# Gated attention and token mixing on one core: one more block of the symmetric score matrix turned by DMA, and transposing transfers joined in sixteens

## The chip, the cores and the metric

One core of one Trainium2 chip runs the whole kernel. The metric is the device time of one execution in microseconds. Engines are named as the profile names them: PE (TensorE), with its weight loads as PEld, DVE (VectorE), ACT (ScalarE), POOL (GpSimd) and SP (SyncE, which issues most DMAs).

## What is computed

There are 8 batches of 3200 rows. The inputs u and v have 256 columns, z has 64, and the weights w_q, w_k are 256x64, w_out is 256x256.

```
scores = z z^T / S                    S = 3200
attn   = relu(scores)^2
x      = u * (attn v)
wq, wk = x w_q, x w_k
W_tok  = wq wk^T / sqrt(64)
out    = relu(W_tok x) w_out
```

The score matrix of a batch is symmetric. A block of attn for rows of one group and columns of another is the transpose of the block on the other side of the diagonal.

## The kernel before, in words

**Tiles.** A batch has 25 tiles of 128 rows, in seven groups: six of 512 rows and a last one of 128 (`widths`, `starts`). For group `gi` and tile `ti` a score tile of 128x512 is two operands of z on the 64 rows of one half of the array (`scores`, L258). Score tiles are made in pairs, one on each half. A pair fills one PSUM tile of two banks; there are two such PSUM tiles, shared with the projections and the mixing (`ps_tile`).

**Two stages of a pair.** `first_stage` (L278) takes relu from PSUM to SBUF on ACT or DVE (g). `second_stage` (L296) squares g into fp16 on ACT or POOL (at). `second_product` (L345) multiplies at by v on PE into `acc`, four matmuls of 64x256 for a tile and a half group. When a group is complete, `gate` (L361) adds the two accumulators and multiplies by u on POOL; a transposing DMA turns x (L400), `projections` (L413) gives the queries and keys (qk), another transposing DMA turns the keys (kx, L436), POOL doubles them (L448), and `heads` (L450) sums k^T x over the batch. `mix` and `proj` then make the output of the batch while the next batch runs.

**Turned blocks.** `is_turned(b, gi, gj)` (L213) says which blocks are made once: group `gi` makes the tiles of the later group `gj`, and a transposing DMA on SP's queue (`turn` in `second_stage`, L330) writes the transposed block into tt, from which group `gj` takes its weights in place of making the scores again. Turned are blocks with `gj` at most two groups after `gi`, and those with the last group (ttl). Batch 0 leaves one out (`SKIP`); `EXTRA`, a list for batches 1 to 7, is empty. Seven homes hold tt blocks (`NHOME`); a block keeps its home until its last tile is read. A transfer carries what one pair made: eight squares of 128x128, or four where only one tile of the pair is turned. z itself is turned for each next batch by four transfers (`ZTURNS`, L153): seven and six squares, for each of two offsets.

**Order.** No hardware scheduler is involved: the kernel is written out by a planner that runs while the program is built. It keeps a clock for PE, DVE, ACT and POOL, and for SP (`sp_at`) and the DMA engines (`dma_at`), with a cost for every operation, and places the next operation by them (main loop from L1029). `move` (L616) files a DMA with the time from which it may go, a due time, SP's issue time and the DMA time; `send` (L619) issues the one that is due first and says when it will have landed. `use_pair` (L681) makes the next pair of scores when a PSUM tile is free and the pair's at tile can be had; `acc_step` (L955) emits the next matmuls of the second product whose rows are ready by the planner's clock. `add_extra` files projections, mixing and heads. At run time engines meet by semaphores alone, and each engine's and queue's instructions go in the order written. So a wrong cost does not make a wrong result; it makes an engine wait.

**Buffers of the square.** at tiles come from a pool of `NAT` = 16, and pair p may be made when pair p - 16 has been read by all its matmuls and its transfers have landed (L1049, `all_used`).

Of the kernel before, what the change touches and what calls it, by code (L numbers as in the profile page):

```python
# [16 lines left out]
def kernel(  # L17
# [33 lines left out]

    NAT = 16
    NX = 7
# [98 lines left out]
    ztimes = []  # L152
    ZTURNS = [(0, 0, 7), (1, 0, 7), (0, 7, 13), (1, 7, 13)]  # L153

# [55 lines left out]
    SKIP = [(0, 2)]  # L210
    EXTRA = []

# [29 lines left out]
    NPAIR = NTILE // 2  # L242
    made, turned = {}, {}
    NHOME = 7
    homes, homes_free = {}, list(range(NHOME))

# [11 lines left out]
    def scores(p, banks=None):  # L258
        assert len(ztimes) >= 4 * tiles[2 * p + 1][0] and p_chunk(p) in z_at, (p, clock, len(ztimes), z_at)
        sc = banks or ps_tile("sc")  # L260
        for h, (b, gi, ti) in enumerate(tiles[2 * p : 2 * p + 2]):
            gs, gw = starts[gi], widths[gi]
            nc.tensor.matmul(  # L263
                out=sc[h][:, 0:gw] if banks else sc[:, h, 0:gw],
                lhsT=z_cols(b, h, ti * P, P),
                rhs=z_cols(b, h, gs, gw),
                start=True,
                stop=True,
            )
        return sc  # L270
# [25 lines left out]
    def second_stage(p, g, ways):  # L296
        at = pat.tile([P, 2 * W], FP16, tag="at", name="at")
        at0 = 0
        parts = pieces(p)
        if len(ways) > len(parts):  # L300
            parts = [(slice(h, h + 1), parts[0][1]) for h in range(2)]
        for (hs, w), on_act in zip(parts, ways * 2):
            n = hs.stop - hs.start
            out = at[:, at0 : at0 + n * w].rearrange("p (n w) -> p n w", w=w)
            if on_act:
                nc.scalar.square(out=out, in_=g[:, hs, 0:w])  # L306
            else:
                nc.gpsimd.tensor_mul(out=out, in0=g[:, hs, 0:w], in1=g[:, hs, 0:w])  # L308
            at0 += n * w
        at0, blocks = 0, []  # L310
        for tile_ in tiles[2 * p : 2 * p + 2]:
            b, gi, ti = tile_
            made[tile_] = (at, at0)
            gj = group_of(ti)
            if is_turned(b, gi, gj):
                blocks.append((b, gi, gj, ti - starts[gj] // P, 1, at0, at0 + widths[gi]))
            at0 += widths[gi]
        if len(blocks) == 2 and blocks[0][:3] == blocks[1][:3] and blocks[1][3] == blocks[0][3] + 1:
            blocks = [blocks[0][:4] + (2, blocks[0][5], blocks[1][6])]

        def turn(b, gi, gj, n0, nn, c0, c1):
            if (b, gi, gj) not in turned:
# [7 lines left out]
            nc.sync.dma_start_transpose(out=out[:, 4 * n0 : 4 * (n0 + nn), :], in_=at[:, c0:c1])  # L330

        return [(x, lambda x=x: turn(*x)) for x in blocks]
# [266 lines left out]
    mixed_at = []  # L599
    MIXES = 10.0  # L600
    MIXES_END = 14.0
# [7 lines left out]
    LANDS = 4.0  # L609
    RING = 2.0  # L610
    SLACK = 1.0
# [83 lines left out]
    def squares():  # L695
        while pending and pending[0][0] <= clock[PE] + 0.3:
# [7 lines left out]
            else:  # L704
                done = give(ACT, ready, 1.06) if by_act else give(POOL, ready, 1.9)
            for (b, gi, gj, _, nn, _, _), turn in second_stage(p, g, ways):
                n = nn * widths[gi] // P
                due = done + {1: 4.0, 2: 9.0}.get(gj - gi, FARDUE)
                out_of[p] = out_of.get(p, 0) + 1
                move(  # L710
                    done + SLACK, due + SLACK, 1.28, 0.21 * n, turn,
                    lambda t, x=(p, b, gi, gj, nn): block_landed(t, *x),
                    lambda x=(b, gi, gj): has_home(*x),
                )
            for x in tiles[2 * p : 2 * p + 2]:
                row_at[x] = done + 0.6

# [14 lines left out]
    def use_keys(b, gi):  # L732
# [17 lines left out]
        if not final:  # L750
            move(
                done + SLACK, done + 10.0, 1.28, 0.21 * n, lambda: turn_keys(b, gi),
                lambda t: at_time(t, lambda: double(b, gi)),
# [63 lines left out]
    def project_out(b, gi, ps, ready):  # L817
# [25 lines left out]
    def batch_begun(b, t):  # L843
        if b + 1 < B:
            t0 = max(t + 6, Z0)
            at_time(t0, lambda: (load_z(b + 1), push(3.0)))
            step = ZSTEP if b else ZSTEP0
            for i, (_, m0, m1) in enumerate(ZTURNS):
                move(
                    t0 + ZWAIT + step * i, t0 + ZDUE + step * i, 1.28, 0.21 * (m1 - m0),  # L850
                    lambda i=i: turn_z(b + 1, i),
# [6 lines left out]
    def v_loaded(b, n0, nn):  # L858
        load_v(b, n0, nn)
        push(2.5)  # L860
        for n in range(n0, n0 + nn):
            v_at[b, n] = dma_at[0] + 5.0

    z_ready = {}

    def z_here(p):
        b = tiles[2 * p + 1][0]
        return not b or z_ready.get((b, 3), 1e9) <= clock[PE]

    def group_begun(b, gi, t):  # L870
        if gi == 0:
            batch_begun(b, t)
        if gi + 1 < NG:
            move(max(t + 2, clock[POOL] + SLACK), t + 7, 0.55, 1.6, lambda: load_u(b, gi + 1))
        elif b + 1 < B:
            move(max(t + 2, clock[POOL] + SLACK), t + 7, 0.55, 1.6, lambda: load_u(b + 1, 0))

    SPARE = 0.5
    BIAS = 0.2
    XDUE = 5.0  # L880
    XWAIT = 2.0
    LATE = 0.5

    def half_done(b, gi, half):
# [10 lines left out]
        if half == halves(gi)[-1]:  # L895
            n = 8 if widths[gi] == W else 2
            move(
                t + SLACK, t + XDUE, 1.28, 0.21 * n, lambda: turn_x(b, gi),
                lambda t: x_landed(t, b, gi), lambda: len(xTs) < NXT,
# [91 lines left out]

    def all_used(p):
        return all(x in used for x in tiles[2 * p : 2 * p + 2])

# [25 lines left out]
    at_time(V3, lambda: (load_first_v(4, 8), give(POOL, clock[PE], 0.6)))  # L1020
    move(10.0, 14.0, 0.55, 1.6, lambda: load_u(0, 0))
    load_weights()
# [3 lines left out]
    done_acc = 0  # L1026
    lead = 140
    turn_about = False
    while groups or work or current["left"]:  # L1029
# [18 lines left out]
        p = produced[0]  # L1048
        able = p < NPAIR and z_here(p) and z_at[p_chunk(p)] <= now and (p < NAT or all_used(p - NAT) and turned_at.get(p - NAT, 0.0) <= now and not out_of.get(p - NAT))  # L1049
        wanted = able and p * total < (done_acc + lead) * NPAIR  # L1050
# [124 lines left out]
```

## Time and profile before

| | |
|---|---|
| median of 3 runs | 774.61 us (774.49 to 777.17) |
| the profiled execution | 773.15 us |
| its span, first to last instruction | 770.9 us |
| matmuls on PE | 12408 |
| score matmuls (L263) | 924 |
| transposing transfers: tt, ttl, xT, kx, zT | 143, 48, 56, 53, 28 |
| DMA packets | 307114, 141.09 MB |

The profile is one execution. A row of a group names the line, the engine, the operation, what it writes and reads, the count, the busy time in us, the mean of one in ns, and the idle time of the engine just before it with what ended it. A row of the chain is a start, a length and what held the end during that time. A row of a window lists its bounds and its length, and then for PE, PEld, DVE, ACT and POOL the busy time with the count of instructions, the granted clock, the share of DMA time and GB/s. Matmuls overlap in the records, so the mean of one matmul (269 ns for 64x256) is longer than the distance to the next.

### The profile page before, as it was taken

Reading aid. Unit: us, or ns where it says so; the run is one execution under the profiler, and the core shown is the slowest. Engines: PE = TensorE matmul, PEld = TensorE weight load, DVE = VectorE, ACT = ScalarE, POOL = GpSimd, SP = SyncE. Lnnn points to the kernel's source line nnn. Section 1 sums busy time; section 2 is a strip of 40 time slices with the busy share of each in tenths; the row PEclk is TensorE's granted clock in tenths of the full one; section 3 lists DMA queues with packets and bytes.
Section 4 is the critical chain, followed back from the end, with each engine's and each line's share of the span. In section 5 each row is a group of like instructions: output and inputs, shape, how many; then the busy total and the mean of one; then the engine's idle time right before and its main releaser. Section 6 shows DMA issues by size and latency. Waiting matters only on the chain.

```text
span 770.9 us, 28221 instructions
## 1 busy us (share of the span) xinstructions
PE 761.7 (99%) x12408; PEld 678.4 (88%) x12408; DVE 510.5 (66%) x537; ACT 561.2 (73%) x647; POOL 591.1 (77%) x496
## 2 busy tenths in 40 slices
PE   8999999999999999999999999999999999999996
PEld 7889998888898888989889988998889989898884
DVE  6775876675787566765677756765667476675645
ACT  7785876778758678875788677877777676777734
POOL 8796788789687778666778687887878887888740
PEclk9999999999999999999999999999999999999998
DMA  8999999999999999999899999999999998979625
GB/s 199 130 187 182 167 204 173 160 212 194 194 162 189 194 209 190 182 213 203 153 190 162 188 231 163 219 145 160 262 156 192 184 190 211 201 143 203 152 84 191
DMA packets 307114, 141.09 MB, mean 183 GB/s; under 512 B 285744, under 2 KB 288432, under 8 KB 306992
## 3 DMA queue, kind: packets, MB, share of 16 engines
q1 hardware_dynamic: 300224, 123.13, 85.0%
q0 software_dynamic: 6624, 15.98, 14.8%
q8 instruction: 97, 1.59, 0.9%
q14 instruction: 25, 0.20, 0.1%
q10 hardware_dynamic: 144, 0.20, 0.1%
HBM read 59.64 MB, written 26.21 MB: 111 GB/s over the span
## 4 chain that ended last, share of the span: by engine, by line
PE 94%; POOL 2%; DVE 1%; DMA 1%; ACT 1%; issue 1%; POOLq 0%; SPq 0%; DVEq 0%; ACTq 0%
PE acc L351 68%; PE sc L263 13%; PE fo L521 6%; PE qk L417 3%; PE qk L455 2%; POOL at L308 2%; PE mx L483 1%; DMA z<-in_z_dram 1%; POOL x_sb L388 1%; DVE g L290 0%; ACT g L286 0%; DVE fo L546 0%; DMA xT_sb<-x_sb 0%; PE hd L455 0%; ACT at L306 0%
## 5 line engine op out<-in xcount | busy, mean ns | idle before, releaser
L351 PE MATMUL acc<-v_sb,at 64*128 64x256 f16 x7344 | 504.7, 269 | 0.0
L308 POOL TENSOR_TENSOR at<-g 128x1024 f16<-128x1024 f32 (+1 forms) x218 | 402.3, 1859 | 71.6 <-ACT g L286 29.1
L351 PEld LDWEIGHTS <-at 64*128 64x128 f16 x7344 | 407.2, 94 | 48.1 <-issue 4.8
L290 DVE TENSOR_SCALAR g<-sc 128x1024 f32<-128x1024 f32 (+2 forms) x285 | 338.5, 1203 | 122.8 <-PE sc L263 114.3
L306 ACT ACTIVATE at<-g 128x1024 f16<-128x1024 f32 (+2 forms) x255 | 257.2, 1023 | 21.8 <-DVE g L290 17.8
L286 ACT ACTIVATE g<-sc 128x1024 f32<-128x1024 f32 (+2 forms) x186 | 183.2, 989 | 76.8 <-PE sc L263 75.0
L388 POOL TENSOR_TENSOR x_sb<-both,u_sb 128x512 f16<-128x512 f32 (+1 forms) x112 | 135.8, 1217 | 81.6 <-DVE both L369 77.7
L263 PE MATMUL sc<-zT 64*128 64x512 f16 x924 | 188.1, 375 | 1.4 <-DVE g L290 0.6
L351 PE MATMUL acc<-v_sb,tt 64*128 64x256 f16 x2272 | 163.4, 269 | 0.0
L351 PEld LDWEIGHTS <-tt 64*128 64x128 f16 x2272 | 126.2, 94 | 10.3
L369 DVE TENSOR_TENSOR both<-acc,both 128x512 f32<-128x512 f32 (+1 forms) x104 | 69.6, 670 | 21.4 <-ACT both L368 17.0
L263 PEld LDWEIGHTS <-zT 64*128 64x128 f16 x924 | 61.2, 94 | 7.6 <-issue 3.9
L368 ACT COPY both<-acc 128x512 f32<-128x512 f32 (+1 forms) x69 | 39.0, 565 | 38.7 <-PE acc L351 36.1
L546 DVE TENSOR_SCALAR fo<-fo 128x1024 f32<-128x1024 f32 (+1 forms) x28 | 32.4, 1166 | 46.6 <-PE fo L521 46.6
L509 ACT ACTIVATE rt<-mx 128x1024 f16<-128x1024 f32 x39 | 39.9, 1024 | 12.6 <-PE mx L483 12.1
L521 PE MATMUL fo<-wo,rt 128*128 128x256 f16 x386 | 46.6, 273 | 0.5 <-ACT rt L505 0.5
L521 PEld LDWEIGHTS <-rt 128*128 128x128 f16 x386 | 36.2, 98 | 8.4 <-issue 3.6
L431 ACT CAST qk<-qk 128x512 f16<-128x512 f32 (+1 forms) x47 | 25.3, 539 | 24.6 <-PE qk L455 20.0
L368 DVE COPY both<-acc 128x512 f32<-128x512 f32 (+1 forms) x35 | 23.6, 674 | 21.2 <-PE acc L351 19.9
L470 DVE TENSOR_TENSOR ha<-qk,ha 128x512 f32<-128x512 f32 x37 | 25.5, 689 | 14.4 <-ACT qk L431 14.1
L551 ACT ACTIVATE fo<-fo 128x1024 f32<-128x1024 f32 (+2 forms) x23 | 22.5, 978 | 16.5 <-PE fo L521 15.8
L417 PE MATMUL qk<-xT_sb,wqk 64*128 64x256 f16 (+1 forms) x404 | 32.3, 265 | 0.0
(55 smaller groups left out, 282.9 us busy)
## 6 DMA issues: line engine op xcount, KB each, us to landing
u_sb<-in_u_dram SPq DMA_DIRECT2D x48, 512.0 KB, 4.8
out_dram<-fo SPq DMA_DIRECT2D x46, 512.0 KB, 5.1
v_sb<-in_v_dram POOLq DMA_DIRECT2D x35, 320.0 KB, 6.0
zn<-in_z_dram POOLq DMA_DIRECT2D x7, 400.0 KB, 7.8
tt<-at SPq DMA_TRANSPOSE x143, 4.7
u_sb<-in_u_dram SPq DMA_DIRECT2D x8, 128.0 KB, 2.9
out_dram<-fo SPq DMA_DIRECT2D x4, 256.0 KB, 3.3
xT_sb<-x_sb SPq DMA_TRANSPOSE x56, 5.4
```

The source lines that it names most:

```text
L263: nc.tensor.matmul(out=sc[h][:, 0:gw] if banks else sc[:, h, 0:gw], lhsT=z_cols(b, h, ti * P, P), rhs=z_cols(b, h, gs, gw), start=True, st ...
L286: nc.scalar.activation(out=g[:, hs, 0:w], in_=part, func=RELU, scale=GSCALE)
L290: nc.vector.tensor_scalar(out=g[:, hs, 0:w], in0=part, scalar1=0.0, scalar2=GSCALE, op0=AOP.max, op1=AOP.mult,)
L306: nc.scalar.square(out=out, in_=g[:, hs, 0:w])
L308: nc.gpsimd.tensor_mul(out=out, in0=g[:, hs, 0:w], in1=g[:, hs, 0:w])
L351: nc.tensor.matmul(out=accs[half, r][:, ds((j % 2) * D, D)], lhsT=weights(b, gi, ti, j)[top(r), :], rhs=vs[b][top(r), ti, :], start=(first ...
L368: copy(out=both[:, 0 : n * D], in_=accs[half, 0][:, 0 : n * D])
L369: nc.vector.tensor_add(out=both[:, 0 : n * D], in0=accs[half, 1][:, 0 : n * D], in1=both[:, 0 : n * D])
L388: nc.gpsimd.tensor_mul(out=xs[b, gi][:, 0:n, :, r, :].rearrange("p n c d -> p (n c) d"), in0=both[:, 0 : n * D].rearrange("p (m d) -> p m ...
L417: nc.tensor.matmul(out=ps[:, r, 0 : n * P], lhsT=wqk[top(r), c, :, :].rearrange("p t h -> p (t h)"), rhs=xTs[b, gi][top(r), 0:n, c, :], st ...
L509: nc.scalar.activation(out=out, in_=part, func=RELU)
L521: nc.tensor.matmul(out=banks[r][:, ds(j * D, D)], lhsT=flat[:, ds((dc * n + j) * P, P)], rhs=wo[:, dc, :], start=(dc == 0 and j == 0), sto ...
```

## The change

- `EXTRA` names block (1, 4): in batches 1 to 7 group 1 makes the tiles of group 4 (the second and the fifth groups), a transfer turns them, and group 4 no longer makes the tiles of group 1.
- Where two pairs that follow each other hold the four tiles of one turned block, they share one at tile of double width, and one transfer of sixteen squares is issued after both are squared. The pool is 10 single tiles and 3 double ones in place of 16 single ones. `prior` says for each pair which earlier pairs must be done with (`has_at` takes the place of `all_used`).
- z is turned by two transfers of thirteen squares in place of four.
- The planner's costs are redrawn: a transposing transfer of n squares takes 0.2 + 0.13 n in place of 0.21 n of DMA time, and so on as in the diff. `XWAIT`, `MIXES`, `lead`, `V1` and `BIAS` are set anew.

```diff
-    NAT = 16
+    NAT = 10
+    NAT2 = 3
...
-    ZTURNS = [(0, 0, 7), (1, 0, 7), (0, 7, 13), (1, 7, 13)]
+    ZTURNS = [(0, 0, 13), (1, 0, 13)]
...
-    EXTRA = []
+    EXTRA = [(1, 4)]
...
+    def block_of(p):
+        rows = [(b, gi, group_of(ti)) for b, gi, ti in tiles[2 * p : 2 * p + 2]]
+        b, gi, gj = rows[0]
+        whole = rows[0] == rows[1] and is_turned(b, gi, gj) and gj < LASTG
+        return rows[0] + (tiles[2 * p][2] - starts[gj] // P,) if whole else None
+
+    twos, prior, at_of, done_at = {}, {}, {}, {}
+    ones = []
+    for p in range(NPAIR):
+        x, y = block_of(p), block_of(p + 1) if p + 1 < NPAIR else None
+        if p - 1 in twos:
+            continue
+        if x and y and x[:3] == y[:3] and (x[3], y[3]) == (0, 2):
+            pairs = sorted(twos)
+            prior[p] = (pairs[-NAT2], pairs[-NAT2] + 1) if len(pairs) >= NAT2 else ()
+            twos[p] = p + 1
+        else:
+            prior[p] = (ones[-NAT],) if len(ones) >= NAT else ()
+            ones.append(p)
...
     def second_stage(p, g, ways):
-        at = pat.tile([P, 2 * W], FP16, tag="at", name="at")
-        at0 = 0
+        if p in twos:
+            at = pat.tile([P, 4 * W], FP16, tag="ats", name="at", bufs=NAT2)
+            at_of[p], at_of[p + 1] = (at, 0), (at, 2 * W)
+        elif p not in at_of:
+            at_of[p] = pat.tile([P, 2 * W], FP16, tag="at", name="at"), 0
+        at, first = at_of[p]
+        at0 = first
...
+        if p in twos:
+            blocks = []
+        elif p - 1 in twos:
+            blocks = [blocks[0][:3] + (0, 4, 0, 4 * W)]
...
-    MIXES = 10.0
+    MIXES = 14.0
...
-    RING = 2.0
+    VLANDS = 4.0
+    RING = 1.5
...
         begun = max(sp_at[0], clock[PE])
-        dma_at[0] = max(dma_at[0], begun) + takes
         sp_at[0] = max(begun + issue, dma_at[0] - RING)
+        dma_at[0] = max(dma_at[0], begun + max(issue, 0.9)) + takes
         if landed:
-            landed(max(sp_at[0], dma_at[0]) + LANDS)
+            landed(dma_at[0] + LANDS)
...
-                    done + SLACK, due + SLACK, 1.28, 0.21 * n, turn,
+                    done + SLACK, due + SLACK, 1.25, 0.2 + 0.13 * n, turn,
...
-        move(done + SLACK, done + 6.0, 0.55, 1.6, stores[0], landed)
+        move(done + SLACK, done + 6.0, 0.45, 1.7, stores[0], landed)
...
-        dma_at[0] = max(dma_at[0], clock[PE]) + takes
+        dma_at[0] = max(dma_at[0], clock[PE] + 2.0) + takes
...
-    V1 = 10
+    V1 = 8
...
-            at_time(t0, lambda: (load_z(b + 1), push(3.0)))
+            at_time(t0, lambda: (load_z(b + 1), push(2.4)))
...
-        push(2.5)
+        push(2.0)
         for n in range(n0, n0 + nn):
-            v_at[b, n] = dma_at[0] + 5.0
+            v_at[b, n] = dma_at[0] + VLANDS
...
-    BIAS = 0.2
+    BIAS = 0.0
     XDUE = 5.0
-    XWAIT = 2.0
+    XWAIT = 7.0
...
-    lead = 140
+    lead = 150
```

The issue and DMA costs of the other transposing transfers, the loads of u and the stores change in the same way.

More of the change, by code (lines that the diff above doesn't have):

```diff
@@ L258, in scores @@
     def scores(p, banks=None):
-        assert len(ztimes) >= 4 * tiles[2 * p + 1][0] and p_chunk(p) in z_at, (p, clock, len(ztimes), z_at)
+        assert len(ztimes) >= len(ZTURNS) * tiles[2 * p + 1][0] and p_chunk(p) in z_at, (p, clock, len(ztimes), z_at)
         sc = banks or ps_tile("sc")
@@ L309, in second_stage @@
             at0 += n * w
-        at0, blocks = 0, []
+        at0, blocks = first, []
         for tile_ in tiles[2 * p : 2 * p + 2]:
@@ L867, in z_here @@
         b = tiles[2 * p + 1][0]
-        return not b or z_ready.get((b, 3), 1e9) <= clock[PE]
+        return not b or z_ready.get((b, len(ZTURNS) - 1), 1e9) <= clock[PE]
     def group_begun(b, gi, t):
@@ L990, in p_chunk, with has_at @@
         return max(c for c, (n0, nn) in enumerate(ZCH) for i in t if n0 <= i < n0 + nn) if p < 12 else 3
-    def all_used(p):
-        return all(x in used for x in tiles[2 * p : 2 * p + 2])
+    def has_at(p):
+        return all(
+            all(x in used for x in tiles[2 * q : 2 * q + 2])
+            and turned_at.get(q, 0.0) <= clock[PE]
+            and not out_of.get(q)
+            for q in prior.get(p, ())
+        )
     blank = wo[:, 0, 0:P]
@@ L1048 @@
         p = produced[0]
-        able = p < NPAIR and z_here(p) and z_at[p_chunk(p)] <= now and (p < NAT or all_used(p - NAT) and turned_at.get(p - NAT, 0.0) <= now and not out_of.get(p - NAT))
+        able = p < NPAIR and z_here(p) and z_at[p_chunk(p)] <= now and has_at(p)
         wanted = able and p * total < (done_acc + lead) * NPAIR
```

17 lines of the change are left out of this document (10 added, 7 removed).

## The prediction

> **What bounds the kernel now.** I read first the share of each engine and the granted clock on the profile's page, then the windows of 100 us, then the list of who waited for whom on TensorE, then the chain that ended last.
>
> ```profile
> span 770.9 us, 28221 instructions
> PE 761.7 (99%) x12408; PEld 678.4 (88%) x12408; DVE 510.5 (66%) x537; ACT 561.2 (73%) x647; POOL 591.1 (77%) x496
> PEclk9999999999999999999999999999999999999998
> ...
> PE 94%; POOL 2%; DVE 1%; DMA 1%; ACT 1%; issue 1%; POOLq 0%; SPq 0%; DVEq 0%; ACTq 0%
> ```
> ```profile
> 100.00:200.00 100.00, 100.00 (x1651) 87.84 (x1649) 65.58 (x70) 75.48 (x84) 84.09 (x70) 1.00 1.02 189
> ...
> 600.00:700.00 100.00, 100.00 (x1650) 91.54 (x1646) 66.68 (x67) 73.96 (x85) 82.60 (x69) 1.00 0.96 187
> 700.00:771.00 71.00, 64.54 (x966) 53.40 (x962) 38.92 (x46) 39.10 (x56) 35.51 (x27) 0.97 0.59 151
> ```
>
> TensorE is busy for 99% of the span at the full granted clock, and from 100 to 700 us it has no hole. "Busy" alone does not say that the matmuls run at their best rate, so the next rows are from the chain: stretches between 30 and 36 us.
>
> ```profile
> 30.46 4.37 PE acc L351 x80
> 34.83 0.22 PE sc L263 x2
> 35.05 0.55 PE acc L351 x10
> 35.59 0.22 PE sc L263 x2
> ```
>
> 80 matmuls of the second product take 4.37 us, 0.0546 us each, and two score matmuls (one pair, on the two row halves) take 0.22 us. About 1650 matmuls stand in each window of 100 us, a mean of 0.061 us with the longer score and projection matmuls in it. So the stream is packed, and the number of matmuls sets the time. Two places are not packed, the first 52 us and the last 25 us. The chain at 45 to 52 us shows the first:
>
> ```profile
> 45.51 0.23 PE sc L263 x2
> ...
> 46.88 1.06 ACT at L306
> 47.93 0.92 ACT g L286
> 48.85 0.04 issue
> 48.90 0.41 PE sc L263 x2
> ```
> ```profile
> PE sc L263 <- DVE g L290: 0.6, 2, 0.4
> PE fo L521 <- ACT rt L505: 0.5, 1, 0.5
> PE ztp L130 <- POOL zd L124: 0.4, 1, 0.4
> PE sc L263 <- ACT g L286: 0.3, 1, 0.3
> PE qq L417 <- DMA xT_sb<-x_sb: 0.2, 1, 0.2
> ```
>
> The second fence is the list of waits on TensorE (its first row, 1.0 us for the memset before the warm-up, is left out). No matmul waits for a transposed block anywhere, and for a DMA only 0.2 us, at the end.
>
> **The change, part by part.**
>
> *The block of groups 2 and 5.* Until now rows 1 and rows 4 (counted from 0) each compute their half of the block. From batch 1 on, group 1 makes it, a transposing transfer turns it, and group 4 reads the result. That drops 4 tiles of 128x512 in each of 7 batches: 28 score matmuls, 14 pairs. In the changed program's order TensorE has 896 score matmuls instead of 924, and all its other matmuls in the same numbers. 14 pairs by 0.22 us from the chain is **3.1 us** less on the engine that sets the end.
>
> ```profile
> L308 POOL TENSOR_TENSOR at<-g 128x1024 f16<-128x1024 f32 x211 | 396.5, 1893 | 70.0 <-ACT g L286 29.1 <-DVE g L290 29.0 <-issue 9.6
> L290 DVE TENSOR_SCALAR g<-sc 128x1024 f32<-128x1024 f32 x278 | 335.2, 1221 | 121.8 <-PE sc L263 113.3 <-POOL at L308 3.3 <-ACT g L286 1.8
> L306 ACT ACTIVATE at<-g 128x1024 f16<-128x1024 f32 x240 | 250.8, 1056 | 21.8 <-DVE g L290 17.8
> ```
>
> The same 14 pairs leave the other engines: 14 evictions of some 1.2 us and 14 squares of 1.06 us (ScalarE) or 1.89 us (GpSimd), at most 14 x (1.22 + 1.89) = 44 us. These engines stand at 66 to 77% and nothing on TensorE ends later for it, so I count nothing.
>
> *Seven more turned blocks, sixteens, and z in two.* Here are the transfers as they are, by tile: issue on SP and issue to landing, shortest, median and longest.
>
> ```profile
> L330 SPq DMA_TRANSPOSE tt<-at x143: 1231/1354/5576, 17.1 to 713.4; - x143
> ...
> DMA to landing us min/median/max: 2.4/4.7/9.8
> ```
> ```profile
> L330 SPq DMA_TRANSPOSE ttl<-at x48: 1193/1262/2715, 26.4 to 723.4; - x48
> ...
> DMA to landing us min/median/max: 2.3/4.7/9.3
> ```
> ```profile
> L436 SPq DMA_TRANSPOSE kx<-qk x53: 1182/1233/2294, 50.2 to 733.7; - x53
> ...
> DMA to landing us min/median/max: 2.3/4.0/9.4
> ```
>
> The order has 251 transposing transfers instead of 328: 80 on tt (77 of sixteen 128x128 squares) for 143, 14 on z for 28, the rest unchanged. 77 issues fewer by 1.3 us is about 100 us less on SP's queue. It is off the path. The squares themselves rise by 7 x 16 = 112.
>
> A transfer of 16 is in no row. From 4 squares (ttl) to 8 (tt) the shortest issue goes from 1.19 to 1.23 us and the shortest landing from 2.3 to 2.4 us, with equal medians of 4.7 us. So one end for a sixteen is no difference, the other is twice an eight: 2.7 us of issue and 9.4 us at the median. I take a value near the first, since the step from 4 to 8 is nearly flat.
>
> Perfetto Trace Analysis in the Trainium skill, section What "DMA-bound" means, says that the DMA slice on the issuing engine's track is descriptor generation, not movement of data. If that grew with the squares, the sixteens would save no time on SP, and the estimate of 100 us there would fall to about nothing. The rows for 4 and 8 speak against such growth, and no row here shows 16. By that rule rival 3 below would weigh about twice as much; the sum is the same, since SP is off the path.
>
> What hides these transfers is distance in TensorE's order. I counted matmuls in the changed program from the last score matmul behind a transfer to the first matmul that reads it. The shortest for a sixteen after batch 0 is 421 matmuls, by 0.0546 us 23.0 us; in the program before the shortest for an eight outside the first two blocks is 471, 25.7 us. The chain to hide is an eviction (1.2), a square (1.9), the other pair's square (1.9 if behind it), an issue and a landing: 9.7 us at the median landing, 14.8 us at the longest of 9.8 us, and 19.8 us if the median doubles and two issues of 2.7 us stand ahead. All are under 23.0 us, so **0**. In batch 0 one sixteen has 327 matmuls, 17.9 us (there an eight had 313 before), which holds up to the longest landing. If the cover is gone, TensorE waits for the difference, once per block.
>
> A joined transfer waits for both pairs' squares, and SP's queue is in order: keys, x, u and stores behind it start later. x has its cover enlarged (a wait of 7 instead of 2 in the planner). The keys are the one whose cover shrinks: the shortest distance from a projection to the first matmul on its turned keys is 273 matmuls before and 191 now, 14.9 and 10.4 us; the median goes from 369 to 331.
>
> ```profile
> L448 POOL COPY kx<-kx 128x128 f16<-128x128 f16 x92 | 24.0, 291 | 2.2 <-DMA kx<-qk 2.2
> L431 ACT CAST qk<-qk 128x512 f16<-128x512 f32 x40 | 23.4, 586 | 23.0 <-PE qk L455 18.5 <-PE qk L417 4.2
> ```
>
> Their chain is a cast of 0.6 us, the landing of 4.0 us (9.4 at the longest) and two copies of 0.3 us: 5.2 us, 10.6 us at worst, without time in queues. I take 0 and keep this as the rival on the slow side.
>
> *Buffers.* 16 square tiles become 10 plus three double ones, the same space. A too small pool would show as ScalarE or GpSimd waiting for TensorE; now the square's largest idle cause is the eviction (29.1 and 29.0 us above). With 44 us of work less I count nothing.
>
> *Redrawn clocks and the first 52 us.* The planner's new costs move the order. What can press TensorE is a pair of PSUM tiles: I looked for places where a PSUM tile is written again less than 1.0 us after it was filled, between 12 and 715 us. There are 14 before and 13 now, seven of them in each between two projections. Four score matmuls in a row at 46 us are the place of the gaps shown above; the list of waits from 40 to 56 us and the group of half squares price it:
>
> ```profile
> PEld L263 <- issue: 1.5, 4, 0.6
> ```
> ```profile
> L308 POOL TENSOR_TENSOR at<-g 128x512 f16<-128x512 f32 x5 | 5.2, 1040 | 0.0
> ```
>
> The weight loads of the scores wait 1.5 us there in four gaps. In the new order that spot is gone, and two like it stand at 19.7 and 20.6 us of matmul time. I count 0.55 us for each, near the longest gap of 0.6. The balance is 1.1 - 1.5 = **-0.4 us**. Its bounds are -1.5 (nothing new) and +1.7: GpSimd does two more half squares before its first gating, and 2.1 us for them could all be exposed.
>
> *The tail* has the same operations in the same sequence: 0.
>
> **Sum.** 3.1 + 0.4 = 3.5 us. The profiled execution took 773.15 us (span 770.9 and 2.25 around it), the median of the three runs is 774.61, 1.46 above. 773.15 - 3.5 = 769.65 us; carried to the median, **771.1 us**. That is 0.45% and just inside 0.5% (3.9 us), which is about what a measurement of this kernel can tell from no change.
>
> **The rivals.**
>
> 1. *More comes back.* The chain gives 6% of the span to others than TensorE, mostly at start and end. If none of the new tight spots at the start costs anything (-1.5 in place of -0.4) and the relieved engines and queue free another 1.0 us there, the time is 771.1 - 2.1 = 769.0 us. For it: GpSimd is the chain at the start. Against: the end is unchanged.
>
> 2. *The gain is used up.* DMA is what becomes tighter.
>
> ```profile
> DMA  8999999999999999999899999999999998979625
> ...
> q1 hardware_dynamic: 300224, 123.13, 85.0%
> ```
>
> The DMA digits are 9 almost throughout. All of q1's 655 us put on its 2130 or so squares gives at most 0.31 us a square, 34 us of DMA for 112 more, against nothing if 4 and 8 cost alike. It stays hidden as long as the distances above hold. If a tenth of it, 3.5 us, comes out at TensorE, the time is 774.6 us.
>
> 3. *Slower: the keys come late.* A key transfer behind two sixteens with doubled issues (5.4 us), landing at the longest (9.4), takes 0.6 + 5.4 + 9.4 + 0.6 = 16.0 us. A quarter of the 53 key blocks, 13, are read within 15.8 us of TensorE's work in the new order. If these are late by 1 us on average, the time is 771.1 + 13 = 784 us. It begins to decide where a key's chain passes 10.4 us and turns the sign where the waits sum to 3.5 us. Against it: 5.2 us is the chain at the median, and SP has fewer issues.
>
> That the change does not do what it says is excluded by the order: 28 score matmuls fewer, 77 sixteens.
>
> **How the numbers follow.** Forecast 0.55 (own range 770.0 to 773.2, by the bounds of the start), rival 1 0.18, rival 2 0.15, rival 3 0.12. Faster by over 0.5% (below 770.7): rival 1 and a third of the forecast, which has half its weight between 770.0 and 771.1: 0.18 + 0.18 = 0.36. Within: the other 0.37 of the forecast and rival 2, 0.52. Slower: 0.12. The range leaves out rival 3 and some of rivals 1 and 2 at their edges: 768.3 to 776.0 us.
>
> **What would show it.** Right: score matmuls x896; TensorE still at 100.00 in the windows from 100 to 700 us; no wait of TensorE on tt or kx; key and tt landings near 4 to 6 us; sixteens' issue near 1.3 us. Wrong: TensorE waiting on kx or on L448's copies (rival 3), an issue of 2.7 us for a sixteen, or gaps in the first 30 us larger than those now at 46 us.

## The result, and the profile after

| | before | changed |
|---|---|---|
| median of 22 runs each, side by side | 775.22 us (773.12 to 780.77) | 780.66 us (775.11 to 794.35) |
| ratio | | 1.0057, 95% interval 1.0031 to 1.0083 |
| profiled execution, its span | 773.15, 770.9 us | 791.02, 789.2 us |

The changed kernel is slower by 0.57%, over the 0.5% of the forecast's cases and outside its range: rival 3 of the prediction is the case that came. Medians are of all executions, while a ratio leaves out those more than 1.5% above the fastest of the same kernel: the traced ones of the changed kernel (ten microseconds above its median) and of e17 below are among these, and e17's ratio rests on two of six. So the trace of the changed kernel says where time can go, and the sizes are taken from the ratios of the experiments.

This is the page of the changed kernel. Against the rows shown of before, the count of matmuls is 28 lower as forecast; TensorE's share falls from 99% to 97%, the fifth slice of the granted clock is 7, and the chain that ended last leaves TensorE for 12% of the span in place of 6%.

```profile
span 789.2 us, 27992 instructions
...
PE 764.2 (97%) x12380; PEld 666.6 (84%) x12380; DVE 491.8 (62%) x527; ACT 545.1 (69%) x624; POOL 597.8 (76%) x503
...
PEclk9999799999999999999999999999999999999999
...
PE 88%; issue 4%; POOL 3%; DVE 2%; DMA 2%; ACT 1%; SPq 0%; POOLq 0%; DVEq 0%; ACTq 0%
```

These are the windows of TensorE alone (bounds, length, busy time and count, granted clock, DMA share, GB/s). Before held 1553 matmuls in the first 100 us and about 1650 in each of the next six. The packed stream now has holes, by far the largest in the first window: 212 matmuls fewer, some 13 us at 0.061 us.

```profile
0.00:100.00 100.00, 88.25 (x1341) 0.95 0.99 157
100.00:200.00 100.00, 100.00 (x1676) 1.00 1.10 187
200.00:300.00 100.00, 97.39 (x1582) 0.98 1.04 185
...
600.00:700.00 100.00, 98.36 (x1624) 1.00 1.04 193
```

These rows say who waited, on TensorE and then on GpSimd (sum, times, longest). Before had no such rows on TensorE, and 2.2 us in two waits where GpSimd now has 47.4 in twelve.

```profile
PE qk L485 <- POOL kx L478: 5.1, 3, 3.8
PE sc L284 <- issue: 4.6, 1, 4.6
PE acc L381 <- POOL at L334: 4.2, 2, 2.6
```
```profile
POOL kx L478 <- DMA kx<-qk: 47.4, 12, 13.6
```

The timeline shows the first of them whole (start, length, engine, line, with the idle time before it in brackets):

```profile
67.58 10.85 SPq L360 DMA_TRANSPOSE tt<-at  x1
...
78.52 1.38 SPq L360 DMA_TRANSPOSE ttl<-at  x1
...
79.99 1.26 SPq L466 DMA_TRANSPOSE kx<-qk  x1
...
86.86 0.52 POOL L478 COPY kx<-kx 128x128 f16<-128x128 f16 x2 [13.63 <-DMA kx<-qk]
...
87.21 1.03 PE L485 MATMUL qk<-x_sb,kx 64*128 64x256 f16 x8 [3.83 <-POOL kx L478]
```

One sixteen holds SyncE for 10.85 us, the keys' transfer goes out behind it, GpSimd stands 13.6 us in front of the copies that double the keys, and TensorE, out of other work, waits for the copies. Now the transfers by tile, to set beside those of before (tt 143 issues of 1231/1354/5576 ns, landing 2.4/4.7/9.8 us; kx landing 2.3/4.0/9.4):

```profile
L360 SPq DMA_TRANSPOSE tt<-at x80: 1254/2827/10847, 16.7 to 729.8; - x80
...
DMA to landing us min/median/max: 2.4/5.8/18.4
```
```profile
L466 SPq DMA_TRANSPOSE kx<-qk x53: 1161/1223/2846, 53.1 to 752.8; - x53
...
DMA to landing us min/median/max: 2.3/4.6/9.3
```

The median issue of a sixteen (a transfer of sixteen squares) is 2.8 us, twice that of an eight. The keys' own transfer is hardly slower than before. What makes the keys late stands ahead of them.

### The profile page after: what moved, and what is told of

The parts are those of the page before. It is cut to its first block, busy times and chain, and to the rows that moved or that the text cites. A ratio compares the mean times of both kernels' runs of the same rounds, so it can differ in the third digit from the quotient of the medians.

```text
span 789.2 us, 27992 instructions
## 1 busy us (share of the span) xinstructions
PE 764.2 (97%) x12380; PEld 666.6 (84%) x12380; DVE 491.8 (62%) x527; ACT 545.1 (69%) x624; POOL 597.8 (76%) x503
## 4 chain that ended last, share of the span: by engine, by line
PE 88%; issue 4%; POOL 3%; DVE 2%; DMA 2%; ACT 1%; SPq 0%; POOLq 0%; DVEq 0%; ACTq 0%
PE acc L381 64%; PE sc L284 12%; PE fo L551 5%; PE qk L447 3%; PE qk L485 2%; POOL at L334 2%; PE mx L513 1%; DVE g L311 1%; DMA kx<-qk 1%; POOL x_sb L418 1%; DMA z<-in_z_dram 1%; ACT g L307 0%; DVE fo L576 0%; DMA xT_sb<-x_sb 0%; DVE both L399 0%
## 5 line engine op out<-in xcount | busy, mean ns | idle before, releaser
L381 PE MATMUL acc<-v_sb,at 64*128 64x256 f16 x7120 | 489.9, 269 | 4.3 <-POOL at L334 4.2
L334 POOL TENSOR_TENSOR at<-g 128x1024 f16<-128x1024 f32 (+2 forms) x225 | 409.7, 1834 | 65.1 <-DVE g L311 50.4
L311 DVE TENSOR_SCALAR g<-sc 128x1024 f32<-128x1024 f32 (+1 forms) x282 | 334.5, 1193 | 190.9 <-PE sc L284 187.9
L381 PEld LDWEIGHTS <-at 64*128 64x128 f16 x7120 | 387.0, 94 | 58.7 <-POOL at L334 5.1
L332 ACT ACTIVATE at<-g 128x1024 f16<-128x1024 f32 (+2 forms) x236 | 238.9, 1027 | 34.8 <-DVE g L311 31.0
L381 PE MATMUL acc<-v_sb,tt 64*128 64x256 f16 x2496 | 186.8, 272 | 0.0
L381 PEld LDWEIGHTS <-tt 64*128 64x128 f16 x2496 | 140.0, 95 | 16.4 <-issue 1.1
L284 PEld LDWEIGHTS <-zT 64*128 64x128 f16 x896 | 59.2, 94 | 11.8 <-issue 7.4
L581 ACT ACTIVATE fo<-fo 128x1024 f32<-128x1024 f32 (+2 forms) x44 | 41.8, 997 | 29.4 <-PE fo L551 29.3
L478 POOL COPY kx<-kx 128x128 f16<-128x128 f16 (+1 forms) x99 | 25.6, 288 | 47.4 <-DMA kx<-qk 47.4
L539 ACT ACTIVATE rt<-mx 128x1024 f16<-128x1024 f32 x36 | 36.8, 1023 | 15.3 <-PE mx L513 15.3
L485 PE MATMUL qk<-x_sb,kx 64*128 64x256 f16 x348 | 29.2, 273 | 5.1 <-POOL kx L478 5.1
```

Of the source, the lines that this page charges most:

```text
L284: nc.tensor.matmul(out=sc[h][:, 0:gw] if banks else sc[:, h, 0:gw], lhsT=z_cols(b, h, ti * P, P), rhs=z_cols(b, h, gs, gw), start=True, st ...
L311: nc.vector.tensor_scalar(out=g[:, hs, 0:w], in0=part, scalar1=0.0, scalar2=GSCALE, op0=AOP.max, op1=AOP.mult,)
L381: nc.tensor.matmul(out=accs[half, r][:, ds((j % 2) * D, D)], lhsT=weights(b, gi, ti, j)[top(r), :], rhs=vs[b][top(r), ti, :], start=(first ...
L485: nc.tensor.matmul(out=ps[:, r, D : 2 * D], lhsT=ks[b, gi][top(r), n, :, :].rearrange("p a h -> p (a h)"), rhs=x_rows(b, gi, n)[top(r), :, :],
L581: nc.scalar.mul(out=flat_out[:, sl], in_=part, mul=FINAL_SCALE)
```

## The experiments

Three theories stand at the start. **K**: the new order leaves the keys too little cover, and they come late. **D**: joined transfers make DMA late as a whole. **B**: the added block is too much for DMA. Later ones are named where they enter. Cover is counted in the written order, in matmuls from a keys' projection (with the heads written right behind it) to the first heads matmul on these keys: fewest 273 and median 369 before, 191 and 331 in the changed kernel.

**e1: more cover for the keys**

```diff
-                lambda t: at_time(t, lambda: double(b, gi)),
+                lambda t: at_time(t + 4.0, lambda: double(b, gi)),
```

> The changed kernel, with the doubling of the turned keys on GpSimd filed 4 us later in the planner (and so the heads that read them). Theory K (the keys land late behind sixteens on the in-order SP queue; GpSimd waits for them in its own order, TensorE starves): the waits of GpSimd for the keys, 47.4 us in the changed kernel's profile, fall under 10 us, TensorE's waits for the copies (5.1 us) go, and the time falls from 780.7 to 771 to 775 us. Theory D (DMA as a whole is late since sixteens hold its rings): other waits stay, time 777 to 782 us. Theory B (the added block is too much traffic): unchanged, 780 us.

Measured: 773.48 us against 776.2 for before in the same session, ratio 0.9987 (0.9960 to 1.0013); cover 255 and 387. The wait on the keys is down to 0.4 us in one time, and TensorE's longest wait is of another kind:

```profile
  DMA kx<-qk: 0.4, 1
```
```profile
PE sc L284 <- ACT g L307: 2.8, 3, 2.1
```

One number in the planner takes back all of the loss, 0.70% or 5.4 us between the two ratios. K holds so far. The sixteens are as slow to issue as in the changed kernel (median 2836 ns on tt), so their slowness alone does not cost the time.

**e2: each sixteen as two eights, same order**

```diff
-            nc.sync.dma_start_transpose(out=out[:, 4 * n0 : 4 * (n0 + nn), :], in_=at[:, c0:c1])
+            for i in range(max(1, nn // 2)):
+                m, c = (2, (c1 - c0) // 2) if nn == 4 else (nn, c1 - c0)
+                nc.sync.dma_start_transpose(
+                    out=out[:, 4 * (n0 + m * i) : 4 * (n0 + m * i + m), :],
+                    in_=at[:, c0 + c * i : c0 + c * i + c],
+                )
```

> The changed kernel with the same order on every engine, each transfer of sixteen squares issued as two of eight directly behind each other. Theory D (the size of a transfer matters by itself): time falls to 771 to 775 us, landings of tt near 4.7 us, the longest issue under 6 us. Theory K: SP holds as long (two issues of 1.3 us or more for one of 2.8), so 778 to 784 us, GpSimd still waits 30 us or more for keys. Theory B: 780 us.

Measured: 794.41 us, ratio 1.0202 (1.0164 to 1.0239). D falls: unjoined, the same order is much worse. K's wait came (55.3 us on the keys), but its time is a miss by 10 us. The time of DMA packets is a little longer than in the changed kernel, which has the same order and the same squares (e2 first):

```profile
q1 hardware_dynamic: 314560, 126.80, 85.5%
```
```profile
q1 hardware_dynamic: 312096, 126.79, 84.9%
```

0.855 of 791.5 us is 677, 0.849 of 789.2 us is 670. The other nine orders with the block and sixteens have 645 to 663 us, so orders differ by more than these two runs do. What makes e2 slower than the changed kernel by their ratios was not shown.

**e3: without the added block**

```diff
-    EXTRA = [(1, 4)]
+    EXTRA = []
```

> The changed kernel without the added block (EXTRA empty), so 28 score matmuls and 3.1 us of TensorE more, 7 sixteens less. Theory B (112 more squares saturate DMA): the waits go and the time is 774 to 776 us. Theories K and D: sixteens and new clocks stay, so waits stay and the time is 780 to 785 us.

Measured: 782.44 us, ratio 1.0071 (1.0043 to 1.0099). B falls: without the block the kernel isn't faster. Its trace has the same stall at the keys:

```profile
POOL kx L478 <- DMA kx<-qk: 21.7, 8, 5.9
```
```profile
PE qk L485 <- POOL kx L478: 2.6, 1, 2.6
```

**e4: the old clocks under the new transfers.** All costs and settings of the planner are put back; sixteens, z in two and the block stay.

```diff
-    MIXES = 14.0
+    MIXES = 10.0
-                    done + SLACK, due + SLACK, 1.25, 0.2 + 0.13 * n, turn,
+                    done + SLACK, due + SLACK, 1.28, 0.21 * n, turn,
...
```

> The changed kernel with sixteens, z in two and the added block, but all planner costs and settings as before (0.21 us a square, the later landing, waits of 2 for x, lead 140 and so on). Theory K in the form that the redrawn clocks took the cover from the keys: time 771 to 775 us. Theory D (sixteens by themselves): 778 us or more.

Measured: 816.36 us, ratio 1.0521 (1.0489 to 1.0552), a miss for K, and within D's open range (778 or more) by its time but not by its reason. The keys wait only 3.8 us in it. The order itself has the holes: run through as the kernel writes it, the planner's own clock of PE stands at 813.7 when the last operation is placed, against 756.9 in the changed kernel and 760.6 in before. At 0.21 us a square it believes a sixteen to hold DMA for 3.4 us, and delays the rows. The clocks can't be parted from the transfers that they describe.

**e8: the redrawn clocks alone**, in the kernel before.

```diff
-    MIXES = 10.0
+    MIXES = 14.0
-                    done + SLACK, due + SLACK, 1.28, 0.21 * n, turn,
+                    done + SLACK, due + SLACK, 1.25, 0.2 + 0.13 * n, turn,
...
```

> The kernel before with all the redrawn clocks, and no more: transfers of eight, z in four, the old set of blocks. The fewest matmuls between a keys' projection and its first use fall to 183 (191 in the changed kernel, 273 before). Theory K+S (the keys come late only where a short cover meets a transfer of sixteen ahead of them on the queue): GpSimd's wait for the keys' transfer stays under 15 us in sum, the time is that of before within 0.5%, 773 to 779. Rival C (the short cover is enough by itself): that wait is over 30 us as in the changed kernel, and the time 779 to 783. Rival E (the redrawn clocks are a gain of their own that the sixteens ate): 769 to 772.

Measured: 794.15 us, ratio 1.0231 (1.0182 to 1.0279). K+S, that the keys need a sixteen ahead to be late, falls: eights do it too. It is rival C, the short cover by itself, and 11 us dearer than the upper end of C's figure. The loss is not planned (the planner's clock ends at 760.1). The clocks alone take the cover to 183, GpSimd waits as in the changed kernel, and TensorE waits 9.7 us for the copies:

```profile
POOL kx L448 <- DMA kx<-qk: 53.5, 15, 7.0
```

**e5: the added block alone**, in the kernel before.

```diff
-    EXTRA = []
+    EXTRA = [(1, 4)]
```

> The kernel before with the added block and nothing else: transfers of eight, z in four, the old clocks. 28 score matmuls fewer and 14 transfers of eight more. The fewest matmuls of the keys are 231 (273 before). If the block is worth its matmuls in any frame (the changed kernel's part that was right): 771 to 773, 3 us under before. Theory S in its form for eights (more transfers hold the queue too): part or all of it comes back, 774 to 777. If the old frame has no DMA room left at all: over 778.

Measured: 790.98 us, ratio 1.0190 (1.0150 to 1.0229): outside the first two cases, in the last one by its time. Whether the chip's DMA had no room was not tested. The keys wait 5.2 us in it. As in e4 the planner writes the holes itself (its clock ends at 780.8), and the windows lose a little everywhere:

```profile
200.00:300.00 100.00, 98.16 (x1600) 1.00 1.10 191
300.00:400.00 100.00, 98.12 (x1630) 1.00 1.09 188
400.00:500.00 100.00, 97.64 (x1572) 1.00 1.08 196
```

So no part that was run alone is a gain: block alone +1.9%, clocks alone +2.3%, transfers and block without clocks +5.2%, all together +0.6%. The sixteens alone and z in two alone were not run.

**e9, e10, e11: e1 without the block (second edit), and e1 with 2 us (shown) and 8 us in place of 4**

```diff
-                lambda t: at_time(t + 4.0, lambda: double(b, gi)),
+                lambda t: at_time(t + 2.0, lambda: double(b, gi)),
-    EXTRA = [(1, 4)]
+    EXTRA = []
```

> The changed kernel with the keys' doubling filed 4 us later, as in e1, and without the added block. Theory K+S: with the keys' stall gone the block is worth its 28 score matmuls in full, so this is 3.1 us over e1, 776 to 777. Rival F (tensor-engine work is not what the end waits for even then; e1 gained by something else): the time is that of e1 within 1 us, 773 to 774.5.

> The changed kernel with the keys' doubling filed 2 us later, half of e1. The fewest matmuls are 219 (191 in the changed kernel, 255 in e1). Theory K+S: the stalls shrink with the cover: GpSimd's wait for the keys' transfer falls from 47 us to between 5 and 25, the time lies between e1 and the changed kernel, 774.5 to 778. Rival R (e1 was a luckier order, the cover has nothing to do with it): wait and time don't follow the cover, 779 or more is as likely as less.

> The changed kernel with the keys' doubling filed 8 us later, twice e1. The fewest matmuls are 301. Theory K+S: the stall is gone at 4 us already, so nothing more comes of it: no wait for keys among the largest, the time that of e1 within 2 us, 772 to 775.5. Rival R: as with 2 us, any time between 773 and 783. Rival G (every matmul of cover is worth something, since transfers of 18 us occur): 769 to 772.

Measured: e9 777.14 us, ratio 1.0015 (0.9990 to 1.0040); e10 778.51, 1.0019 (0.9985 to 1.0053); e11 779.87, 1.0055 (1.0020 to 1.0090). The block's 28 matmuls, forecast at 3.1 us, are worth 2.2 us by the ratios of e9 and e1, each known to some 2 us; so this agrees with the forecast without showing it. e10 lies between as K has it, with 17.7 us of waits on the keys (its median is half a microsecond above the range given). e11 is a miss. Its plan is longer (the planner's clock ends at 760.9, against 757.0 in e1). It has no wait on the keys, but one stall of another kind near 330 us, where the square's tiles were not free because sixteens had not landed:

```profile
POOL at L334 <- DMA tt<-at: 9.6, 3, 5.6
ACT at L332 <- DMA tt<-at: 8.1, 1, 8.1
```

More cover at the keys than needed brings nothing, and the late sixteens then show at another place. This is what theory S took up: the planner charges a sixteen's issue with 1.25 us and it takes 2.8, so whatever has the shortest cover behind it is late. Its rival R is that each order draws a stall or two of its own by chance.

**e13, e12, e15: the true issue charged (first edit); the same with e1; e1 with a longer landing (second edit)**

```diff
-                    done + SLACK, due + SLACK, 1.25, 0.2 + 0.13 * n, turn,
+                    done + SLACK, due + SLACK, 1.25 if n < 16 else 2.8, 0.2 + 0.13 * n, turn,
-    LANDS = 4.0
+    LANDS = 6.0
```

> The changed kernel, where the planner charges SyncE 2.8 us for the issue of a sixteen (the traced median is 2.83) in place of 1.25, and nothing else. The fewest matmuls from a keys' projection to their first use become 233 (191 in the changed kernel, 255 in e1, 219 in e10). Theory S (the queue of SyncE is held by sixteens for longer than the planner knows, and whatever has the shortest cover is then late: the keys in the changed kernel, squares' buffers in e11): the order leaves more room behind sixteens, GpSimd's wait for the keys' transfer falls under 20 us, time 773 to 777. Rival R (each order draws its own one or two stalls by chance): any time between 773 and 783. Rival K (only the filed cover of the keys counts): as e10 by its distance, 776 to 779.

> e1 (keys' doubling filed 4 us later) with the true 2.8 us issue of a sixteen charged too. The fewest matmuls of the keys are 279 (255 in e1). Theory S: no stall of TensorE over 3 us anywhere, time 771 to 774, at or under e1. Theory K: as e1, 773.5. Rival R: 773 to 783.

> e1 with the landing of every transposing transfer assumed 6 us after its place in the planner's DMA clock in place of 4. The fewest matmuls of the keys are 287. Theory S: like e12, more room for all transfers, 771 to 774. Theory K: as e1, 773.5. Rival R: 773 to 783.

Measured: e13 777.15 us, ratio 1.0024 (0.9995 to 1.0052), keys' wait 22.5 us; e12 775.40, 1.0010 (0.9984 to 1.0037), 4.8 us; e15 775.39, 1.0016 (0.9983 to 1.0050), 11.4 us. The true charge helps by itself, to the edge of what S gave in time and just past it in the wait (under 20 us); K's 776 to 779 by the cover of 233 holds it as well. With e1 neither charge adds anything: e12 and e15 are over the figures of S and of K, and R alone is not excluded by them. Planned room has a price in these orders (the planner's clock ends at 759.9 in both, against 757.0 in e1).

**e17, e18: the keys earlier in SyncE's queue, without and with e1's cover** (2 us in e18)

```diff
-                done + SLACK, done + 10.0, 1.25, 0.2 + 0.13 * n, lambda: turn_keys(b, gi),
+                done + SLACK, done + 6.0, 1.25, 0.2 + 0.13 * n, lambda: turn_keys(b, gi),
```

> The changed kernel where the keys' transfer is due 6 us after its cast in place of 10, so that the planner places it further ahead in SyncE's queue, and nothing else. The cover stays as short as in the changed kernel or shorter: fewest matmuls 191 (191), median 307 (331). Theory Q (the late keys are time in SyncE's queue behind other transfers): the median wait from the cast to the issue falls under 3 us from 3.8, the longest under 13 us from 17.8, GpSimd's wait for the keys' transfer falls well under 47 us, time 774 to 778. Theory K (the cover decides, the queue does not matter): wait and time as in the changed kernel or worse, 780 to 785. Rival R (every order has one or two stalls of its own): 773 to 783, with the largest stall at another tile.

> e1 (keys' doubling filed 4 us later) with the keys' transfer due 2 us after its cast in place of 10. The fewest matmuls of the keys are 249 (255 in e1), the median 391 (387). Theory Q: queue short and cover long, no wait for keys worth naming; the block's 3.1 us comes out against the kernel before: 770 to 773. Theory K: as e1, 772 to 775. Rival R, or the other transfers pushed back by the keys come late in their place: 775 to 783.

Theory Q is that the late keys are time in SyncE's queue behind other transfers. Measured: e17 791.56 us, ratio 1.0086 (1.0055 to 1.0117); e18 782.66, 1.0054 (1.0023 to 1.0086). Q's figures are missed: in e17 the median wait ahead of the keys' issue did fall, to 2.9 us, but the longest was 15.9 (under 13 was expected), and with the cover as short as in the changed kernel GpSimd waits as long as there. As the longest waits stayed, e17 doesn't show what a short queue would do.

```profile
  DMA kx<-qk: 48.7, 15
```

e18 has the cover and still one large stall. Its timeline on SyncE, GpSimd and TensorE, and the windows of TensorE around it:

```profile
328.60 16.49 SPq L360 DMA_TRANSPOSE tt<-at  x2
...
345.20 2.06 SPq L466 DMA_TRANSPOSE kx<-qk  x1
...
349.19 0.52 POOL L478 COPY kx<-kx 128x128 f16<-128x128 f16 x2 [9.01 <-DMA kx<-qk]
...
349.54 1.03 PE L485 MATMUL qk<-x_sb,kx 64*128 64x256 f16 x8 [5.79 <-POOL kx L478]
```
```profile
338.00:342.00 4.00, 4.00 (x58) 1.00 1.35 69
342.00:346.00 4.00, 1.75 (x32) 1.00 1.28 108
346.00:350.00 4.00, 0.46 (x6) 0.79 0.97 105
350.00:354.00 4.00, 4.00 (x40) 0.50 1.01 223
354.00:358.00 4.00, 4.00 (x63) 0.85 1.08 148
358.00:362.00 4.00, 4.00 (x72) 1.00 1.08 291
```

Two sixteens hold SyncE for 16.5 us, and the keys land 24.1 us after their cast; the fewest matmuls of cover, 249, are 13.6 us. R is right in this: an order with sixteens can draw such an event.

**Together.** The rows are ordered by cover. The keys' wait is GpSimd's (in e1 by the row of the tile), the longest landing that of tt. The wait, the landing and the time in the fourth column are of the traced execution, the ratio is of the runs. e4 and e5, whose orders hold planned holes, are left out (their keys wait 3.8 and 5.2 us).

| run | cover, fewest and median | keys' wait, us | traced execution, us | longest landing, us | ratio |
|---|---|---|---|---|---|
| before | 273, 369 | 2.2 | 773.15 | 9.8 | 1 |
| e8, eights | 183, 325 | 53.5 | 792.36 | 10.3 | 1.0231 |
| e3 | 187, 315 | 21.7 | 783.02 | 12.8 | 1.0071 |
| e2, two eights | 191, 331 | 55.3 | 793.29 | 11.4 | 1.0202 |
| changed | 191, 331 | 47.4 | 791.02 | 18.4 | 1.0057 |
| e17 | 191, 307 | 48.7 | 791.38 | 13.3 | 1.0086 |
| e10 | 219, 333 | 17.7 | 777.43 | 13.5 | 1.0019 |
| e13 | 233, 363 | 22.5 | 776.89 | 11.3 | 1.0024 |
| e18 | 249, 391 | 10.3 | 781.24 | 16.8 | 1.0054 |
| e1 | 255, 387 | 0.4 | 774.88 | 11.6 | 0.9987 |
| e9, no block | 269, 377 | 14.6 | 778.08 | 11.7 | 1.0015 |
| e12 | 279, 399 | 4.8 | 775.78 | 15.6 | 1.0010 |
| e15 | 287, 401 | 11.4 | 773.91 | 14.5 | 1.0016 |
| e11 | 301, 403 | none | 780.81 | 11.2 | 1.0055 |

Under 200 matmuls of cover the keys wait 21 us or more and the kernel is slower; above, the wait is under 23 us and the ratio within 0.25% of before, but for e11 and e18 with their one event each. The traced executions go with their own waits: 791 to 793 us where the keys wait over 47 us, 777 to 783 with 14 to 23, 773 to 776 with less, apart from the same two. So a wait belongs to its own execution and not to the median of the kernel: the changed kernel's 47.4 us go with 791 us, not with 781. No order beats the kernel before by more than its interval; e1 is the fastest.

## Why the prediction was wrong, step by step

*28 score matmuls, 3.1 us:* the count is right (x896); the time agrees, with 2.2 us between the ratios of e9 and e1, but is not clear of their intervals. It comes out only where the order has room for the block's transfers, as e5 shows: there the block alone costs 1.9%, 15 us.

*Other engines relieved, buffers, tail: 0.* Nothing of the loss was traced to them. In the traces of before and of the changed kernel no engine waits for a transfer on tt to free a tile of the square. With the keys in time such waits do appear: ScalarE stands 2.8 us in e1 and 8.1 us in e11. So 0 for the buffers is right for this loss, and too little for what the change could gain.

*Sixteens, issue near an eight's:* **wrong size**. I took a value near "no difference"; the other end, 2.7 us, is what came: the median is 2.83. Over all 77 the shortest is 1.32 us, against 1.23 for an eight, so the shortest issues said nothing of the rest. Part of it is the size: with no other transfer of the kernel out (issued and not yet landed), three sixteens of the changed kernel took 1.63, 2.07 and 2.94 us, two eights of before 1.24 and 1.25. Part is what is still out: with three other transfers out the medians are 3.10 and 1.26 us, with four 4.61 and 2.63. Two eights in e2, at their median of 1.37, hold SyncE for 2.7 us as well, so the 100 us less on SyncE did not come: all transposing issues sum to 553 us before and 532 in the changed kernel. The shortest issues and the medians of 4 and 8 are flat and could not show it; the longest, 2.7 and 5.6 us, double, and were the row to take. By Perfetto Trace Analysis in the Trainium skill, section What "DMA-bound" means, the slice on the issuing engine is descriptor generation. The shortest issues (1.19, 1.23 and 1.32 us for four, eight and sixteen squares) don't bear out a cost by the square, while from eight to sixteen the medians would have come out right by it.

*Sixteens, cover of 23 us: 0:* right for tt itself, no matmul waited for a sixteen. But the landing, counted up to 9.8 us, reached 18.4, and in e1 and e11 sixteens held up the squares.

*Keys, "5.2 us, 10.6 us at worst, without time in queues", 0:* **the step that failed.** The queue was most of the chain already. Pairing the 53 casts with the 53 keys' transfers in the trace of before, the issue starts 6.1 us after the cast at the median and 15.3 at the longest, and the keys have landed after 11.8 and 21.9 us, not 5.2 and 10.6. So 273 matmuls, 14.9 us, were not ample. They were enough because each block had the cover that its own chain needed: the landing that comes closest to its first heads matmul is still 4.7 us ahead of it. In the changed kernel's trace the keys land 8.7 us after the cast at the median, which is sooner than before, but up to 24.6 us after it, the cover is shorter, and three landings are only 0.4 us ahead of the matmul that had to wait for them. The redrawn clocks by themselves bring the short cover (e8: 183). I had the number that mattered, 273 to 191, and set it against a chain without its longest part. This was rival 3, given 0.12. Its mechanism is right (a key's chain over 10.4 us, behind a held queue), though e8 shows that the queue need not hold sixteens. Its 784 us, for thirteen blocks late by 1 us, is above the 780.66 measured, and the trace has three waits of TensorE, 5.1 us in sum, instead.

*The start, -0.4:* not visible. e1, with the same block, clocks and transfers, has 1563 matmuls in its first 100 us against 1553 (first row below); the changed kernel loses far more there, to the keys at 87 us among others.

*Rival 2, DMA used up:* not as priced. By q1's share its packets take 670 us in the trace of the changed kernel, 645 in that of e1 and 655 in before's, so the squares did not bring 34 us more, and no wait of TensorE on tt came out.

*What would show it:* both marks named for "wrong" were there, TensorE behind the copies of kx and 2.7 us for a sixteen.

What is left of e1 to the forecast's 3.5 us: its trace has one wait for an eviction on ScalarE at 140 us, and the window there has 62 matmuls fewer than before's, 3.8 us (second row). The eviction was late because ScalarE, in its own order, had first stood 2.8 us in front of a square whose tile a sixteen still held:

```profile
0.00:100.00 100.00, 96.47 (x1563) 1.00 1.04 175
100.00:200.00 100.00, 97.85 (x1589) 0.98 1.06 193
```
```profile
138.09 1.06 ACT L332 ACTIVATE at<-g 128x1024 f16<-128x1024 f32 x1 [2.83 <-DMA tt<-at]
...
139.05 1.01 ACT L307 ACTIVATE g<-sc 128x1024 f32<-128x1024 f32 x1
...
140.11 0.48 PE L284 MATMUL sc<-zT 64*128 64x512 f16 x2 [2.15 <-ACT g L307]
```

*Open:* why a single sixteen is now and then held for 10.9 us. It was seen in the traces of the changed kernel and of e18; no run tried to set it off.

TensorE's wait of 4.6 us put down to "issue" stands in the same stretch, at 74 to 78 us. The page names nothing that ended it, but the packets of the queue that loads instructions do:

```profile
q8 instruction: 97, 1.59, 0.9%
```

These are 97 packets of 16 KB, one for about 255 matmuls and weight loads of TensorE. One of them starts at 75.9 us, 16.9 us after the one before it, where 7.6 us is the median, and TensorE goes on 2.6 us after its start. In the traces of e4, e9, e12, e15 and e17 the one wait of each that is over 0.5 us and put down to "issue" also ends 2.3 to 2.6 us after the start of such a packet. So TensorE most likely had no instructions, because their load came late in the same jam; no run tested it.

## What to carry to other kernels

A chain that ends in an in-order queue is measured from its producer's end to its landing, queue included, before its cover is called ample. When transfers are joined, take the median under load, not the shortest, for the new size, and ask what stands behind it in the queue. A planner's costs hold for the transfers that they were fitted to: here each half of the change alone was worse than both.

## What the runs showed of the hardware that was not expected

- Joining two transposing transfers of eight into one of sixteen goes with less DMA time for the same squares, by q1's share of the span: with the added block 645 to 670 us in ten traces with sixteens, 677 and 683 in the two with eights (e2, e5); without it 635 and 647 (e3, e9) against 655 and 668 (before, e8). How much of it is the joining can't be told from orders that differ by up to 25 us among themselves. Each sixteen holds its queue twice as long as an eight (2.8 us against 1.35 at the median).
- Every run with sixteens has a longest tt landing of 11.2 to 18.4 us, the four with eights 9.8 to 11.4.
- Short jams: in e18 from 338 to 350 us DMA moved 69 to 108 GB/s where some 190 are usual, with its engines counted as busy (0.97 to 1.35), and a load of v from GpSimd's queue, issued at 329.5, landed with them after 15.6 us. The changed kernel has 105 and 74 GB/s from 72 to 80 us, around its first stall, and there the load of TensorE's instructions seems to be held up with the rest.
- A stall costs more than its length. After the 5.8 us wait in e18 the granted clock was 0.50 for 4 us and 0.85 for the next 4: 40 and 63 matmuls where 66 is the mean of a packed stretch (1650 in 100 us), some 1.8 us more. TensorE: Matmul & The Clock Gate in the Trainium skill, in its part on the HAM clock gate, says that one idle window of about 3.4 us brings the clock to half until a busy one has passed. This trace agrees, but shorter waits did it too: after 2.15 us in e1 and 2.61 us in the changed kernel (at 258 us) the clock was at half for 3.4 us.
